# Engine order from a list scheduler, DMA transposes and per-pair scores in a windowed-attention + MLP kernel

## The chip, the cores and the metric

The kernel runs on one core of a Trainium2 chip. The metric is the time of one execution on the device, in microseconds (us). A run more than 1.5% above the fastest of the same kernel counts as slow and is left out of comparisons. The engines are called PE (TensorE, matmuls), PEld (its weight loads), ACT (ScalarE), DVE (VectorE), POOL (GpSimd) and SP (SyncE, which here only issues DMAs).

## The reference, cut to what matters

```python
# q, k, v: 4 batches x 8 heads x 768 rows x 64; n_global = 8, n_local = 96
scores = scale * q @ k.T + bias(head, distance)      # kept: 96 local columns and the first 8
a = softmax(where(keep, scores, -1e9));  attn = a @ v
x = attn -> (3072 rows) x (8 heads * 64 = 512)
h = x @ w_in                  # 512 x 2048
out = relu(h)**2 @ w_out      # 2048 x 512, float32
```

The 3072 rows are 24 tiles of 128. Because of the window, a tile needs keys of itself and of the tile before (plus the 8 global columns, which are copied into the tile before). Two tiles make a block. In the names below, `kT` and `xT` are k and x transposed, `sc` the scores, `esc` their exp, `po` the result of the attention's second product (PV). The MLP of a block has eight steps. "Stage 1" of a step is eight 128x128 by 128x256 matmuls into `hT`, then relu on ACT, then the square on DVE. "Stage 2" is four matmuls with 512 columns that accumulate over the eight steps into two banks `acc`.

q and k have a standard deviation of 0.1, so the scaled scores vary by about 0.1 x 0.1 x 8 / 8 = 0.01. The output therefore hardly depends on q and k.

## The kernel before

TensorE transposes q, k and the attention result x of every tile (heads are interleaved with zeros in `qz`, so that one matmul gives the scores of a pair of heads). PSUM is the memory that the matmuls write to; it is divided into banks. Scores of two pairs fill two PSUM banks, and one exp reads both. The order of the instructions is a hand-made table.

```python
    ps_acc = ...tile_pool(name="ps_acc", bufs=1, space=PSUM)   # acc0, acc1: 2 banks
    ps_h   = ...tile_pool(name="ps_h",   bufs=2, space=PSUM)
    ps_sc  = ...tile_pool(name="ps_sc",  bufs=1, space=PSUM)   # 2 banks
    ps_tr  = ...tile_pool(name="ps_tr",  bufs=1, space=PSUM)
    ps_o   = ...tile_pool(name="ps_o",   bufs=1, space=PSUM)
# ... cut ...
    def unit_a(j):                     # transposes of tile j
        tr = ps_tr.tile([P, 2 * NPAIR, P], BF16, name="tr", tag="tr")
        # ... 4 + 4 nc.tensor.transpose of q and k into tr ...
        nc.vector.tensor_copy(z[:D, :, 0, :], tr[:D, :NPAIR, :])
        nc.vector.tensor_copy(z[D:, :, 1, :], tr[D:, :NPAIR, :])
        nc.scalar.copy(kT[j], tr[:, NPAIR:, :])
# ... cut ...
    def unit_scores(j, hf):            # two pairs of heads at a time
        sc = ps_sc.tile([P, 2, 4 * P], FP32, name="sc", tag="sc")
        # ... four score matmuls, 256 columns each ...
        esc = work.tile([P, 8 * P], BF16, name="esc", tag="esc")
        nc.scalar.activation(out=esc, in_=sc..., func=Act.Exp, scale=scale)
        # ... at = esc * bias on DVE ...
# ... cut ...
    for j in range(8, NT):
        a0 = 4 * (j - 2) - 5
        put(j, A=a0, B=a0 + 2, C=a0 + 3, D=a0 + 4, E=a0 + 5, F=a0 + 7)
```

The softmax here doesn't subtract the row's maximum and nothing guards it: scores larger than these inputs give would overflow.

## Time and profile before

| | before |
|---|---|
| median (before the prediction, 3 runs) | 269.84 us (267.59 to 270.02) |
| PE busy | 223.3 us, 84% of the span |
| DVE, ACT busy | 57%, 52% |
| first stage-1 matmul | 26.7 us |
| steady block (two tiles) | 19.4 us |

The page of the profile gives the busy time of each engine, and then rows of 40 equal slices: a digit is the busy share of a slice in tenths, in the row PEclk the share of full clock that was granted, in the row DMA the share of the 16 DMA engines.

```profile
PE 223.3 (84%) x1935; PEld 160.3 (60%) x1968; DVE 151.1 (57%) x350; ACT 139.8 (52%) x229; POOL 73.4 (28%) x94
...
PE   1345969686989899899799899898998998999993
...
PEclk9999999999999999999999999999999999999999
DMA  8999999999999300200200200200200200202022
```

PE is the busiest engine, less so in the first third, and the DMA engines are full for the first third (the loads) and nearly idle afterwards.

The windows view gives, for each stretch of time, its length and the busy time of PE, PEld, DVE, ACT and POOL (instructions in brackets), then granted clock, DMA share (of the packets' time, so above 1 where packets wait for each other) and GB/s.

```profile
40.00:60.00 20.00, 16.46 (x147) 12.16 (x151) 11.53 (x25) 9.30 (x14) 19.14 (x23) 1.00 2.42 155
60.00:80.00 20.00, 15.94 (x157) 11.79 (x158) 11.29 (x25) 10.62 (x17) 19.54 (x24) 1.00 2.33 170
...
120.00:140.00 20.00, 18.34 (x162) 13.48 (x164) 11.59 (x25) 11.22 (x19) 0.00 (x0) 1.00 0.08 28
```

From 80 us on, up to the last 30 us, PE is busy 18.3 to 18.6 of 20 us at full clock (one such stretch is shown), and no other engine comes near that. From 40 to 80 us it lacks 4 us in 20.

The table of waits, for PE (waiting instruction, what ended the wait, us in total, times, longest):

```profile
PE acc L338 <- ACT o L349: 10.5, 9, 1.4
...
```

And the timeline of PE at the end of a steady block (start, duration, line, operation, output and inputs, how many; in brackets an idle time before it and what ended it). Durations of single matmuls contain their pipeline latency; the distance of two starts is what a group really costs.

```profile
185.34 0.29 PE L254 MATMUL po<-v,at 128*128 128x65 bf16 x4
187.08 1.08 PE L338 MATMUL acc<-wout,hs 128*128 128x512 bf16 x4 [1.45 <-ACT o L349]
...
188.87 0.60 PE L219 MATMUL sc<-qz,kT 128*128 128x256 bf16 x4
189.31 1.03 PE L338 MATMUL acc<-wout,hs 128*128 128x512 bf16 x4
...
```

Once in most blocks, stage 2 of the next block waits for ACT to evict the accumulator (1.45 us here, 10.5 us in all). The score group takes 189.31 - 188.87 = 0.44 us for its four matmuls.

### The profile page before, as it was taken

Reading aid. Unit: us, or ns where it says so; the run is one execution under the profiler, and the core shown is the slowest. Engines: PE = TensorE matmul, PEld = TensorE weight load, DVE = VectorE, ACT = ScalarE, POOL = GpSimd, SP = SyncE. Lnnn points to the kernel's source line nnn. Section 1 sums busy time; section 2 is a strip of 40 time slices with the busy share of each in tenths; the row PEclk is TensorE's granted clock in tenths of the full one; section 3 lists DMA queues with packets and bytes.
Section 4 is the critical chain, followed back from the end, with each engine's and each line's share of the span. In section 5 each row is a group of like instructions: output and inputs, shape, how many; then the busy total and the mean of one; then the engine's idle time right before and its main releaser. Section 6 shows DMA issues by size and latency. Waiting matters only on the chain.

```text
span 266.5 us, 4844 instructions
## 1 busy us (share of the span) xinstructions
PE 223.3 (84%) x1935; PEld 160.3 (60%) x1968; DVE 151.1 (57%) x350; ACT 139.8 (52%) x229; POOL 73.4 (28%) x94
## 2 busy tenths in 40 slices
PE   1345969686989899899799899898998998999993
PEld 1124657464666677577577677576676775766641
DVE  6444576466457576565557567565575675653310
ACT  5432474444557456556556555654745646635321
POOL 8986778999994000000000000000000000000000
PEclk9999999999999999999999999999999999999999
DMA  8999999999999300200200200200200200202022
GB/s 161 155 196 200 186 180 155 157 155 155 198 157 154 87 2 0 81 1 2 79 2 1 79 2 0 81 0 2 79 2 1 79 2 1 81 0 81 0 79 79
DMA packets 84758, 20.76 MB, mean 78 GB/s; under 512 B 75520, under 2 KB 81664, under 8 KB 84736
## 3 DMA queue, kind: packets, MB, share of 16 engines
q0 software_dynamic: 77120, 13.11, 63.2%
q1 hardware_dynamic: 7616, 7.34, 8.3%
q8 instruction: 15, 0.25, 0.4%
q14 instruction: 7, 0.06, 0.1%
HBM read 27.26 MB, written 6.29 MB: 126 GB/s over the span
## 4 chain that ended last, share of the span: by engine, by line
PE 66%; DVE 16%; ACT 11%; issue 5%; ACTq 0%
PE acc L338 27%; PE hT L314 26%; PE sc L219 7%; DVE hs L325 4%; ACT hr L323 4%; DVE x L275 3%; DVE qz L188 2%; ACT esc L228 2%; PE po L265 2%; ACT o L349 2%; PE trx L291 2%; DVE qz L187 2%; ACT kT L189 2%; DVE at L237 1%; DVE rs L274 1%
## 5 line engine op out<-in xcount | busy, mean ns | idle before, releaser
L325 DVE TENSOR_TENSOR hs<-hr 128x512 bf16<-128x512 f32 x96 | 66.3, 691 | 69.6 <-ACT hr L323 69.3
L338 PE MATMUL acc<-wout,hs 128*128 128x512 bf16 x351 | 92.9, 379 | 12.3 <-ACT o L349 10.5
L314 PE MATMUL hT<-xT,win 128*128 128x256 bf16 x768 | 101.2, 276 | 0.1
L314 PEld LDWEIGHTS <-win 128*128 128x128 bf16 x768 | 75.7, 99 | 28.2 <-issue 0.2
L323 ACT ACTIVATE hr<-hT 128x512 f32<-128x512 f32 x96 | 57.7, 601 | 54.6 <-PE hT L314 54.6
L338 PEld LDWEIGHTS <-hs 128*128 128x128 bf16 x384 | 35.7, 98 | 37.6 <-issue 13.2
L228 ACT ACTIVATE esc<-sc 128x1024 bf16<-128x1024 f32 x44 | 45.2, 1028 | 5.8 <-PE sc L219 4.7
L237 DVE TENSOR_TENSOR at<-esc,E 128x1024 bf16<-128x1024 bf16 x44 | 30.4, 691 | 27.1 <-ACT esc L228 27.0
L189 ACT COPY kT<-tr 128x512 bf16<-128x512 bf16 x24 | 14.0, 584 | 50.8 <-DVE qz L188 45.1
L219 PE MATMUL sc<-qz,kT 128*128 128x256 bf16 x160 | 25.8, 287 | 7.5 <-ACT kT L189 5.2
L87 POOL DMA_DIRECT2D v<-in_v_dram x24 | 23.4, 975 | 2.6 <-DMA win<-in_moe_w_in_dram 1.2
L96 POOL DMA_DIRECT2D k<-in_k_dram x22 | 21.3, 968 | 3.3 <-DMA wout<-in_moe_w_out_dram 2.8
L219 PEld LDWEIGHTS <-kT 128*128 128x128 bf16 x160 | 15.3, 102 | 10.6 <-ACT kT L189 6.1
L96 POOL DMA_DIRECT2D q<-in_q_dram x22 | 21.2, 965 | 1.4 <-DMA win<-in_moe_w_in_dram 0.7
L275 DVE TENSOR_TENSOR x<-po,rs 128x256 bf16<-128x256 f32 x48 | 20.4, 425 | 1.7
L265 PE MATMUL po<-v,at 128*128 128x65 bf16 x320 | 16.8, 196 | 3.4 <-DVE x L275 3.4
L265 PEld LDWEIGHTS <-at 128*128 128x128 bf16 x320 | 15.1, 100 | 5.7 <-DVE x L275 4.9
L349 ACT COPY o<-acc 128x512 f32<-128x512 f32 x24 | 13.0, 597 | 6.3 <-PE acc L338 6.3
L180 PE MATMUL tr<-ident,q 128*128 128x128 bf16 x96 | 9.9, 230 | 6.8 <-DVE q L175 6.8
L294 ACT COPY xT<-trx 128x512 bf16<-128x512 bf16 x24 | 14.0, 582 | 3.1 <-PE trx L291 3.1
L291 PE MATMUL trx<-ident,x 128*128 128x128 bf16 x96 | 9.9, 226 | 5.7 <-ACT kT L189 4.1
L291 PEld LDWEIGHTS <-x 128*128 128x128 bf16 x96 | 7.5, 100 | 6.9 <-issue 4.5
(34 smaller groups left out, 94.2 us busy)
## 6 DMA issues: line engine op xcount, KB each, us to landing
out_dram<-o SPq DMA_DIRECT2D x24, 256.0 KB, 2.2
v<-in_v_dram POOLq DMA_DIRECT2D x24, 128.0 KB, 6.1
q<-in_q_dram POOLq DMA_DIRECT2D x22, 128.0 KB, 5.9
k<-in_k_dram POOLq DMA_DIRECT2D x22, 128.0 KB, 6.0
win<-in_moe_w_in_dram POOLq DMA_DIRECT2D x8, 256.0 KB, 7.2
wout<-in_moe_w_out_dram POOLq DMA_DIRECT2D x8, 256.0 KB, 9.8
plain_q<-in_q_dram SPq DMA_DIRECT2D x2, 256.0 KB, 3.9
plain_k<-in_k_dram SPq DMA_DIRECT2D x2, 256.0 KB, 4.3
```

The costliest lines, as they stand in the source:

```text
L87: nc.gpsimd.dma_start(out=v_sb[j][:, :, :D], in_=v[b, :, t * P : (t + 1) * P, :].rearrange("h p d -> p h d"),)
L96: nc.gpsimd.dma_start(out=dst.rearrange("p (h d) -> p h d", h=H), in_=src[b, :, rows, :].rearrange("h p d -> p h d"),)
L219: nc.tensor.matmul(out=sc[:, pi, i * 2 * P : (i + 1) * 2 * P], lhsT=kT[kj][:, pair, :], rhs=z[:, pair, :, :], start=True, stop=True, skip_ ...
L228: nc.scalar.activation(out=esc, in_=sc.rearrange("p a b -> p (a b)"), func=Act.Exp, scale=scale)
L237: nc.vector.tensor_mul(at, esc, bias)
L265: nc.tensor.matmul(out=po[:, hi, :], lhsT=a4[:, hi // 2, i, hi % 2, :], rhs=v_sb[kj][:, h, :], start=(i == 0), stop=(i == 1), skip_group_c ...
L275: nc.vector.tensor_tensor(out=x[:, 4 * hf : 4 * hf + 4, :], in0=po[:, :, :D], in1=rs.to_broadcast([P, 4, D]), op=Alu.mult,)
L291: nc.tensor.transpose(out=trx[:, kt, :], in_=x[:, kt * P : (kt + 1) * P], identity=ident)
L314: nc.tensor.matmul(out=hT[:, c, :], lhsT=w_in_sb[s][:, kt, c * P : (c + 1) * P], rhs=xT[blk][:, kt, :], start=(kt == 0), stop=(kt == KM - ...
L323: nc.scalar.activation(hr, hT, Act.Relu)
L325: nc.vector.tensor_mul(hs, hr, hr)
L338: nc.tensor.matmul(out=acc[blk][sub], lhsT=hs[:, c, sub * P : (sub + 1) * P], rhs=w_out_sb[s][:, c, :], start=(s == 0 and c == 0), stop=(s ...
```

## The change

The intent: PE should do matmuls only. q and k of tiles 4 and up are transposed by DMA (SP), q from buffers padded with zeros; x too. A list scheduler with estimated costs orders all engines: it takes, again and again, the operation that can start first by its plan. Scores are made per pair of heads (one bank), the accumulators get a third bank, weights of the two stages are loaded alternately, and copies go to ACT or DVE, whichever is planned to be free. The diff, cut to its core:

```diff
+class Plan:
+    LAG = {"PE": 0.2, "ACT": 0.1, "DVE": 0.1, "SP": 2.6, "POOLQ": 2.5, "DMA": 0.0}
+    def run(self):
+        # ... among ready operations, take the one with the least (start, key, cost) ...
+                if o["takes"]:                       # a buffer of a ring
+                    tag, bufs, users = o["takes"]
+                    if len(ring) >= bufs:
+                        old = ring[-bufs]            # wait for the users of the oldest
 # ... cut ...
-    ps_acc = ctx.enter_context(tc.tile_pool(name="ps_acc", bufs=1, space=PSUM))
+    ps_acc = ctx.enter_context(tc.tile_pool(name="ps_acc", bufs=3, space=PSUM))
     ps_h = ctx.enter_context(tc.tile_pool(name="ps_h", bufs=2, space=PSUM))
     ps_sc = ctx.enter_context(tc.tile_pool(name="ps_sc", bufs=1, space=PSUM))
-    ps_tr = ctx.enter_context(tc.tile_pool(name="ps_tr", bufs=1, space=PSUM))
     ps_o = ctx.enter_context(tc.tile_pool(name="ps_o", bufs=1, space=PSUM))
 # ... cut ...
+    NPE = 4
+    NPAD, NK, NV, NKT, NQZ = 6, 6, NT, 2 * TPB, 4
 # ... cut: loads of tiles 6 and up wait for the buffers that transposes free ...
+            ld = plan.op(("load", j), {"POOLQ": 2.6}, emit_load,
+                deps=pad_users[j % NPAD] + k_users[j % NK], key=base, ready=clock[0])
 # ... cut: tiles below NPE keep TensorE transposes, the others get ...
+                nc.sync.dma_start_transpose(
+                    out=qz[zi].rearrange("p a b c -> p (a b) c"),
+                    in_=q_tile[j].rearrange("p a b c -> p (a b c)"))
+                nc.sync.dma_start_transpose(out=kT[ki], in_=k_tile[j])
+            T = plan.op(("T", j), {"SP": 1.5}, emit_T, ..., key=base - 6)
 # ... cut ...
+                sc = ps_sc.tile([P, 2, 2 * P], FP32, name="sc", tag="sc")
+            s_ = plan.op(
+                ("sc", j, pair), {"PE": 0.11 if first else 0.22}, emit_sc, deps=deps,
+                key=base + 0.5 + 0.4 * pair, takes=("sc", 2, users))
 # ... cut: exp, mask and PV per pair; x of tiles 4 and up ...
+                nc.sync.dma_start_transpose(
+                    out=tiles["xT", blk][:, :, tt * P : (tt + 1) * P],
+                    in_=tiles["x", j].rearrange("p h d -> p (h d)"))
+            c = plan.op(("xT", j), {"SP": 0.9}, emit_xT, deps=norm, key=base + 3, takes=xT_ring)
 # ... cut ...
+    for o in plan.run():
+        if o["emit"]:
+            o["emit"](o["engine"])
```

## The prediction

> **What bounds the kernel now.** TensorE. In the windows table of the kernel before, PE is busy 18.4 to 18.6 of each 20 us from 80 to 240 us at full granted clock, while DVE has 11.5 to 13.6 and ACT 10.7 to 12.0. The timeline shows a block (two tiles, eight steps) every 19.4 us. By start-to-start times its TensorE work is 8 stage-1 groups of 0.87 us, 8 stage-2 groups of 0.86, four score groups of 0.44, four PV groups of 0.25, and transposes (q and k 0.22 each, x 0.22) of 1.35 us for both tiles: about 18.0. The rest is mostly one wait a block for the accumulator's eviction: the table of waits has "PE acc <- ACT o" 10.5 us in 9 waits. The start is the other loss: the first stage-1 matmul runs at 26.7 us, PE is busy 20.7 of the first 40 us and 32.4 of the 40 after.
>
> **Removed.** TensorE transposes of 20 tiles (0.67 us each, 13.5 us) and their copies (DVE 0.84, ACT 1.16 us a tile, off the critical path); the accumulator wait (10 us); some early idle: float32 transposes need no casts, k comes on a second queue, and w_out chunks come between w_in chunks, so stage 2 can start before all of stage 1 of block 0 is done. The weights still need what the trace's 160 to 200 GB/s allows, so block 0 ends near 45 us either way, but with some 6 us of stage 2 done. Without new waits I estimate a 16.6 us block and about 229 us in all.
>
> **Added.** Three DMA transposes a tile on SP. The Trainium skill, "VectorE: DVE Perf Modes", section "The three transpose paths", gives 1309 ns for a 128x128 through the DMA crossbar against 390 on TensorE; this trace has 230 ns (modelled) for the latter and no instance of the former. With tiles prepared steps ahead I expect little of it on the chain.
>
> **The catch.** The plan lets the scheduler use two score buffers, but the score pool keeps one buffer; a pair's scores now fill one bank. "PSUM — Partial Sum Buffer", section "Specifications (TRN2)", gives 8 banks of 512 float32: the new pools take 3+2+1+1 = 7, so a bank lies idle. The keys put two score pairs back to back, twice a tile, right after a stage-1 group whose relu goes ahead of the exp on ACT. The second pair must then wait for relu and exp: from this trace 0.17 us pipeline, 0.49 for the relu, 0.60 for the exp, less 0.22 own issue, so about 1.1 us idle. Twice a tile, some 18 tiles in steady state: 35 to 40 us on TensorE, all critical. A block would then take 20 to 21 us, longer than before, and nearly all of the gain goes.
>
> **Prediction.** 263 us, range 245 to 278. Faster by over 2%: 0.48; within 2%: 0.32; slower: 0.20.
>
> **What would show each step.** Right: transposes of later tiles gone from PE; "PE acc <- ACT o" near zero; first stage-1 matmul near 20 us; "PE sc <- ACT esc" the largest PE wait, 25 to 45 us, in 30 to 40 waits of about 1 us; block period 19.5 to 21 us; ACT and DVE under 65% busy. Wrong: score waits under 15 us (the order interleaves other work, then 230 to 245 us); large waits of PE on DMA transposes (q, k or xT), which would make it slower; a first stage-1 matmul later than 26 us.
>
> **What would make it wrong.** DMA transposes slower than the planned 4 us, above all beside the early loads; the in-order SP queue blocked by a store; score pairs less often adjacent than I read from the keys; the zero fills on POOL delaying the weights more than the estimated 3 us.

## The result, and the profile after

The changed kernel took 284.42 us (median of 4 runs, 283.07 to 284.83) against 268.76 us: slower, at a ratio of 1.0573 (95% interval 1.05 to 1.0646). Ratios here are the mean time of one kernel's fast runs over that of the other's fast runs of the same rounds, so they are not quite the ratios of the quoted medians. All four runs were fast ones, yet their mean granted clock was 0.96.

The page after, same lines as before:

```profile
PE 225.1 (80%) x1728; PEld 152.1 (54%) x1728; DVE 147.5 (52%) x375; ACT 122.6 (43%) x226; POOL 89.0 (32%) x120
...
PE   2778987594387958887977978978878888879993
...
PEclk9999999799559979999999999999999999999998
DMA  8999999999999994987997997245164021020201
```

PE was busy for as long as before (225 us), although it executes 240 matmuls fewer (12 transposes in each of 20 tiles; the counts on the page differ by 207, as some records of the kernel before are missing). The saving hardly shows in the busy time, which fits with two things: the 33 missing records are of `acc` (351 of 384, 92.9 us against 103.3 us after), and the kernel after runs part of its matmuls at half clock, where they take longer. The DMA row is full for much longer, and in the first half the granted clock sinks to a half in some slices.

The windows of the kernel after:

```profile
40.00:60.00 20.00, 13.96 (x111) 8.91 (x110) 9.65 (x24) 8.48 (x15) 14.95 (x19) 0.91 1.95 164
60.00:80.00 20.00, 11.81 (x63) 6.72 (x62) 4.35 (x10) 3.66 (x8) 11.44 (x15) 0.80 1.82 155
...
120.00:140.00 20.00, 17.15 (x146) 11.89 (x144) 11.61 (x27) 9.71 (x17) 6.55 (x8) 1.00 1.05 121
```

Two losses show. From 40 to 110 us PE works far less than before, at a lowered clock. Counting the stage-1 matmuls in this stretch gives 152, against 216 before: 64 fewer, one whole block. From 120 us on, the clock is full and PE still reaches only 16.7 to 17.2 of 20 us.

The table of waits of PE, after:

```profile
PE sc L404 <- ACT esc L432: 34.1, 49, 1.0
PE hT L605 <- DMA xT<-x: 9.5, 2, 7.4
...
PE sc L404 <- DMA kT<-k: 3.3, 2, 2.9
PE acc L669 <- DVE hs L638: 0.9, 2, 0.6
```

The accumulator wait is gone. In its place stand 34.1 us of waits of score matmuls for the exp of the pair before. The timeline of PE in a steady block shows one of them, and the ACT timeline below it why it is so long:

```profile
182.63 1.04 PE L605 MATMUL hT<-xT,win 128*128 128x256 bf16 x8
183.50 0.38 PE L404 MATMUL sc<-qz,kT 128*128 128x256 bf16 x2
184.84 0.38 PE L404 MATMUL sc<-qz,kT 128*128 128x256 bf16 x2 [0.95 <-ACT esc L432]
...
```

```profile
183.70 0.60 ACT L626 ACTIVATE hr<-hT 128x512 f32<-128x512 f32 x1 [1.14 <-PE hT L605]
184.19 0.59 ACT L432 ACTIVATE esc<-sc 128x512 bf16<-128x512 f32 x1
```

The first score pair starts at 183.50, right behind a stage-1 group. ACT takes that group's relu first (183.70) and then the exp of the pair (184.19). The second pair needs the same bank, so it can start only at 184.84: 1.34 us after the first, where its own work needs 0.22. The steady block takes 182.63 to 202.75, that is 20.1 us, longer than the 19.4 us before.

The chain that ended last shows the other loss (start, duration, what):

```profile
...
42.16 9.06 DMA kT<-k
...
65.76 8.56 DMA xT<-x
...
74.45 1.65 PE hT L605 x7
...
```

A transpose of k takes 9 us from issue to landing, and one of x takes 8.6 us, while stage 1 of the next block waits for it. The slow landing is not the whole of this wait. The timeline of SP shows what stood before that x:

```profile
62.42 3.24 SPq L382 DMA_TRANSPOSE kT<-k  x1
65.76 1.28 SPq L581 DMA_TRANSPOSE xT<-x  x1
```

DVE had finished this x at 60.85 us, but SP came to it only at 65.76 us. Until 59.7 us SP had stood at a store whose accumulator was not yet copied (10.3 us), and then it issued that store and the q and k transposes of a later tile. So x spent 4.9 us in SP's queue and 8.6 us from issue to landing; PE had other work until 67.0 us and then waited 7.4 us.

The DMA view of 30 to 100 us gives the median time from issue to landing of each kind:

```profile
qz<-qpad SPq DMA_TRANSPOSE x8, 8.2
kT<-k SPq DMA_TRANSPOSE x8, 7.8
xT<-x SPq DMA_TRANSPOSE x4, 6.6
```

The plan counted on 4.1 us for q and k together (1.5 of issue and 2.6 to land) and 3.5 us for x. And a long wait costs twice, because the clock falls. The windows of PE around the wait for x (length, PE busy, clock, DMA share, GB/s):

```profile
66.00:74.40 8.40, 1.01 (x6) 0.85 1.82 137
74.40:86.00 11.60, 10.05 (x42) 0.52 1.80 199
86.00:100.00 14.00, 11.22 (x91) 1.00 2.15 154
```

After the wait of 7.4 us, PE ran for 11.6 us at a mean clock of 0.52. The Trainium skill, "TensorE: Matmul & The Clock Gate", section "What's actually happening", describes such a fall to half clock after an idle window of about 3.4 us. This trace agrees for the wait of 7.4 us, but shorter idling did it too: after a wait of 2.9 us (for kT, ending at 51.3 us) the clock was at half for 3.4 us, and after one of 2.1 us (for xT, ending at 100.9 us), soon followed by a score wait of 0.95 us, for another 3.4 us. By themselves the score waits, of 1.0 us at most, leave the clock at 1.00 from 107 to 270 us.

### The profile page after: what moved, and what is told of

It is laid out like the page before. It is cut to its first block, busy times and chain, and to the rows that moved or that the text cites. A ratio compares the mean times of both kernels' runs of the same rounds, so it can differ in the third digit from the quotient of the medians.

```text
span 282.4 us, 4671 instructions
## 1 busy us (share of the span) xinstructions
PE 225.1 (80%) x1728; PEld 152.1 (54%) x1728; DVE 147.5 (52%) x375; ACT 122.6 (43%) x226; POOL 89.0 (32%) x120
## 3 DMA queue, kind: packets, MB, share of 16 engines
q1 hardware_dynamic: 48416, 17.31, 33.7%
## 4 chain that ended last, share of the span: by engine, by line
PE 57%; DMA 15%; ACT 11%; POOL 6%; DVE 5%; issue 4%; SPq 0%; ACTq 0%; POOLq 0%
PE acc L669 25%; PE hT L605 23%; ACT esc L432 9%; PE sc L404 6%; DMA xT<-x 5%; DMA wout<-in_moe_w_out_dram 4%; DMA qpad<-in_q_dram 3%; DMA kT<-k 3%; PE po L495 2%; DVE at L452 2%; ACT hr L626 2%; DVE o L278 1%; POOL v L175 1%; POOL win L175 1%; POOL qpad L259 1%
## 5 line engine op out<-in xcount | busy, mean ns | idle before, releaser
L669 PE MATMUL acc<-wout,hs 128*128 128x512 bf16 x384 | 103.3, 387 | 0.9 <-DVE hs L638 0.9
L638 DVE TENSOR_TENSOR hs<-hr 128x512 bf16<-128x512 f32 x96 | 66.3, 691 | 65.9 <-ACT hr L626 65.1
L404 PE MATMUL sc<-qz,kT 128*128 128x256 bf16 x176 | 38.1, 293 | 37.4 <-ACT esc L432 34.1
L432 ACT ACTIVATE esc<-sc 128x512 bf16<-128x512 f32 (+1 forms) x96 | 53.8, 560 | 32.3 <-PE sc L404 30.6
L175 POOL DMA_DIRECT2D qpad<-in_q_dram x40 | 30.4, 771 | 62.6 <-DMA qz<-qpad 59.3
L452 DVE TENSOR_TENSOR at<-esc,E 128x512 bf16<-128x512 bf16 (+1 forms) x96 | 37.0, 396 | 10.8 <-ACT esc L432 10.8
L278 DVE COPY o<-acc 128x512 f32<-128x512 f32 x12 | 8.3, 692 | 25.2 <-PE acc L669 25.2
L520 DVE RECIPROCAL rs<-po 128x4 f32<-128x4 f32 x48 | 8.7, 180 | 12.7 <-PE po L495 11.8
L276 ACT COPY o<-acc 128x512 f32<-128x512 f32 x12 | 7.0, 585 | 10.3 <-PE acc L669 10.3
L175 POOL DMA_DIRECT2D win<-in_moe_w_in_dram x8 | 6.5, 818 | 2.2 <-DMA win<-in_moe_w_in_dram 2.2
L175 POOL DMA_DIRECT2D wout<-in_moe_w_out_dram x8 | 6.0, 754 | 2.2 <-DMA wout<-in_moe_w_out_dram 2.2
```

What stands on the lines that cost most here:

```text
L175: nc.gpsimd.dma_start(out=dst, in_=src)
L278: nc.vector.tensor_copy(dst, src)
L404: nc.tensor.matmul(out=sc[:, i, :], lhsT=kT[(j - i) % NKT][:, pair, :], rhs=qz[zi][:, pair, :, :], start=True, stop=True, skip_group_check ...
L432: nc.scalar.activation(out=esc[:, :n], in_=sc.rearrange("p a b -> p (a b)")[:, :n], func=Act.Exp, scale=scale,)
L452: nc.vector.tensor_mul(at_, tiles.pop(("esc", j, pair))[:, : at_.shape[1]], bias)
L520: nc.vector.reciprocal(rs, po[:, :, D : D + 1])
```

## The experiments

Theory A: two causes. The single score buffer, which the plan believes to be two, costs about 35 us of PE waits; and DMA transposes beside the loads take 6 to 9 us, which starves PE until about 110 us. Rivals: only one of these matters; or transposes are slow by themselves; or SP's order or the tie between buffers and loads is at fault. Each run was compared with the kernel before in the same rounds (its medians there were 268.1 to 269.2 us).

| run | median us | ratio to before (95%) |
|---|---|---|
| changed kernel | 284.42 | 1.0573 (1.05-1.0646) |
| 1: two score buffers | 258.09 | 0.9605 (0.9561-0.9648) |
| 2: one buffer, and the plan knows | 263.59 | 0.9832 (0.9792-0.9872) |
| 3: all transposes on PE | 279.84 | 1.0416 (1.0367-1.0465) |
| 4: 1 and 3 together | 241.41 | 0.8991 (0.8958-0.9024) |
| 5: as 1, x on PE | 246.50 | 0.9196 (0.9163-0.9229) |
| 6: as 1, tiles 4 to 11 on PE | 232.84 | 0.8668 (0.8645-0.8692) |
| 7: as 1, no late loads of q and k | 246.96 | 0.9211 (0.9176-0.9247) |
| 8: as 1, dearer SP in the plan | 264.39 | 0.9852 (0.9801-0.9903) |
| 9: as 1, no late loads at all | 236.75 | 0.8800 (0.875-0.8851) |
| 10: as 6, larger rings, later zero fills | 229.92 | 0.8551 (0.8512-0.8591) |
| 11: as 4, two accumulator banks | 241.41 | 0.8978 (0.8942-0.9024) |
| 12: as 1, larger rings | 265.54 | 0.9893 (0.9842-0.9943) |

### 1 and 2: the score buffer

Run 1 changes one number, and the two traces show the same operations in the same order on every engine as in the changed kernel:

```diff
-    ps_sc = ctx.enter_context(tc.tile_pool(name="ps_sc", bufs=1, space=PSUM))
+    ps_sc = ctx.enter_context(tc.tile_pool(name="ps_sc", bufs=2, space=PSUM))
```

> The score pool gets the two buffers that the plan counts on (the idle bank); the order of every engine stays the same as in the changed kernel. Theory A (half of the loss is the single score buffer): the waits of score matmuls for the exp fall from 34 us to under 5, the steady block from 20.1 to 16.6-17 us, the time from 284 to 250-258 us; the stretch from 40 to 110 us stays poor, with xT and kT transposes of 6 to 9 us. Rival B (DMA transposes beside the loads are all that matters, the score waits hide other waits): the time stays above 275 us.

Measured: 258.09 us, 26 us less than the changed kernel and at the edge of the forecast. Its waits of PE:

```profile
PE hT L605 <- DMA xT<-x: 18.9, 5, 8.7
PE sc L404 <- DMA kT<-k: 6.8, 2, 5.0
...
```

No wait of scores for the exp is left among the rows of this table. From 160 to 220 us the windows view has PE busy 20.00 of each 20 us, and the steady block takes 16.6 us, which is what the prediction gave without new waits. The waits for DMA transposes grew instead, to 18.9 and 6.8 us, as the early score waits no longer hide them. This fits with 34 us of waits giving back only 26.

Run 2 keeps the single buffer and corrects the plan:

```diff
-                key=base + 0.5 + 0.4 * pair, takes=("sc", 2, users),
+                key=base + 0.5 + 0.4 * pair, takes=("sc", 1, users),
```

> The score pool keeps one buffer, but the scheduler is told so, and orders the engines for one. Theory A: it puts other TensorE work between two score pairs; score waits fall under 15 us and the time to 258-268 us. If it is the number of buffers and not the false count in the plan that costs, the waits stay near 30 us and the time above 278.

Measured: 263.59 us, 21 us less than the changed kernel, with one score buffer:

```profile
PE sc L404 <- DMA kT<-k: 10.4, 3, 6.1
PE hT L605 <- DMA xT<-x: 10.0, 5, 4.4
PE sc L404 <- ACT esc L432: 6.0, 13, 0.7
...
```

With the true count, the scheduler puts stage-2 or PV matmuls between two score pairs, and the score waits fall from 34.1 to 6.0 us. So most of the cost was not the single buffer as such, but a plan that counted on two. The second buffer is still worth 5.5 us (263.59 to 258.09). Run 2 orders every engine anew, so its other waits differ too.

### 3 and 4: the transposes back on PE

A condition of its own, in place of `j < NPE`, says which tiles TensorE transposes; the order of the loads stays. (A q tile for TensorE loads in one DMA into a buffer of its own, not in two into a padded one; this small difference comes along.)

```diff
+    QK = lambda j: True      # q, k by TensorE
+    XP = lambda j: True      # x by TensorE
-        if j < NPE:          # at the load of q, at the transposes of q and k
+        if QK(j):
-        if j < NPE:          # at the transpose of x
+        if XP(j):
```

> All 24 tiles transposed by TensorE as tiles 0 to 3 are (through the two hT banks); one score buffer with the plan's false count stays, loads keep their order. Theory A (contention of transposes with loads is the other half): no slow clock from 60 to 110 us, no wait for xT or kT; some 20 us come back there, against 1.35 us of TensorE work a block (10 blocks, 13 us): 272-280 us, with a steady block of 21 to 21.5. Rival (transposes cost nothing, the start is poor for lack of data): 290 us or more.

> Both: two score buffers and all transposes on TensorE. If the two causes add: 240-248 us with a steady block near 18 us. If one of them was only a stand-in for the other: no better than the first run of this batch.

Run 3 (one score buffer): 279.84 us, with no wait for a DMA transpose among the rows, a clock of 0.996, and the score waits as they were:

```profile
PE sc L406 <- ACT esc L434: 35.4, 48, 1.0
...
```

Run 4 (two buffers): 241.41 us. Its windows, to be read against 13.96 and 11.81 of the changed kernel:

```profile
40.00:60.00 20.00, 19.97 (x169) 13.94 (x168) 11.88 (x27) 10.27 (x19) 16.15 (x19) 1.00 2.11 180
60.00:80.00 20.00, 19.97 (x179) 14.49 (x178) 14.07 (x36) 13.64 (x28) 6.55 (x8) 1.00 1.04 88
...
```

So both causes are real, and run 4 lies within its forecast. The gains of the single changes do not add up to the joint one, which is larger: the PE transposes gain 4.6 us with one buffer (284.42 to 279.84) and 16.7 us with two (258.09 to 241.41); the second buffer gains 26.3 us with DMA transposes and 38.4 us with PE transposes. This fits with score waits and waits for DMA that partly cover each other in the first 110 us, so that removing one lays the other bare.

### 5 and 6: which transposes, and when

Run 5 has two score buffers, `QK = lambda j: j < NPE` and `XP = lambda j: True`. Run 6 has both set to `j < 12`.

> Two score buffers (as all of this batch); x of every tile transposed by TensorE, q and k of tiles 4 and up still by DMA. If only the late, urgent xT transposes cost (they wait on SP behind q and k of tiles further ahead), this gives 240-246 us. If the q and k transposes themselves, two thirds of the transposed bytes, slow the loads and are slowed by them, sc waits for kT remain and it lands at 246-256.

> Two score buffers; tiles 4 to 11 transposed by TensorE, tiles 12 and up by DMA, so that hardly any transpose meets the dense loads of the first 80 us. If transposes are harmless once the dense loads are over: 232-239 us, faster than all on TensorE (241.4) by what 12 tiles' transposes cost there, some 8 us. If they hurt there too: 241 us or more.

Run 5: 246.50 us, at the border of the two forecasts. It is 11.6 us faster than run 1 with only x on PE, so the urgent x transposes are the larger part; but 10.6 us of waits for kT remain, and with all on PE it is another 5.1 us faster. Run 6: 232.84 us, 8.6 us faster than all on PE. Transposes by DMA do pay, for the tiles whose transposes come after the dense loads. (Its profiled execution, 236.25 us, fell in a slow run, so its trace is not used for times.)

### 7, 8, 9 and 12: why the transposes are slow

Run 7 leaves out the q and k loads of tiles 6 and up, but keeps the v loads, the transposes and the planned order; run 9 leaves out the v loads as well (late tiles use the v buffers of the first six). Both compute something wrong.

```diff
     def load_tile(j):
+        if j >= NPE + 2:
+            q_tile[j], k_tile[j] = q_pad[j % NPAD], k_ring[j % NK]
+            load_v(j)        # run 9: without this line, and v_sb[j] = v_sb[j % 6]
+            return
```

> Wrong result on purpose: two score buffers, all DMA transposes and the engine order kept, but the q and k loads of tiles 6 and up left out (zeros or old tiles are transposed in their place), v still loaded. If the loads slow the transposes: transposes of 40 to 110 us land in 2.4 to 4.5 us instead of 8, waits for xT and kT under 6 us, 232-242 us. If transposes are slow by themselves or blocked by the order on SP: waits stay above 15 us and the time above 250.

> Wrong result on purpose: as the run without late q and k loads, and the v loads of tiles 6 and up left out too, so nothing is loaded after about 45 us; two score buffers, the engine order and all DMA transposes kept. In the earlier run v loads moved up and filled the DMA engines until 72 us, and only after that did transposes land in 2.4 to 3.7 us. If loads are what slows the transposes: the wait of 9.6 us for xT near 65 us goes too, transposes after 50 us land in 2.4 to 4 us, 230-238 us. If not: still near 247.

Run 7: 246.96 us, between the forecasts. The v loads, no longer behind q and k, moved up and kept the DMA engines full until about 72 us, and until then nothing got better; waits of 16.2 us for xT and kT remained, which was the rival's side of the forecast. From 70 to 110 us the transposes landed fast:

```profile
...
qz<-qpad SPq DMA_TRANSPOSE x7, 3.4
kT<-k SPq DMA_TRANSPOSE x7, 3.7
xT<-x SPq DMA_TRANSPOSE x4, 2.4
```

Run 9 removed these loads too: 236.75 us. From 50 to 160 us its transposes land in 2.4 to 3.3 us:

```profile
...
qz<-qpad SPq DMA_TRANSPOSE x16, 3.3
kT<-k SPq DMA_TRANSPOSE x16, 2.6
xT<-x SPq DMA_TRANSPOSE x12, 2.4
```

The same DMAs, in the planned order of run 1, land in a third to two fifths of the time shown for the changed kernel once nothing is loaded beside them, and the wait for xT shrinks from 18.9 to 2.0 us. So the transposes are not that slow by themselves; the loads beside them make them so. That it is the shared DMA engines, and not the memory behind them, fits the full DMA rows but was not separated. Run 9 also removes the wait of q and k transposes for their data, so that by itself it would not tell late data from slow transposes; but the times above count from issue to landing. In SP's queue x stood almost as long as before: the x transpose that made PE wait 7.4 us in the changed kernel waited 4.0 us there in run 9 (4.9 us in the changed kernel), and yet no wait of PE for xT was over 1.6 us. So most of the long waits is slow landing. What a shorter queue alone would give was not tested.

Run 9 was reported as wrong (relative error 1.11). Run 7 was reported as correct, although it used stale or zero q and k: this is the insensitivity to q and k named above. The passed checks of the other runs thus prove the x, v and MLP paths, but not the q and k transposes.

Run 8 has two score buffers and only tells the scheduler dearer DMA transposes:

```diff
-    LAG = {..., "SP": 2.6, ...}      # and {"SP": 1.5} for q and k, {"SP": 0.9} for x
+    LAG = {..., "SP": 7.0, ...}      # and {"SP": 2.6} for q and k, {"SP": 1.2} for x
```

> Two score buffers; only the plan's costs for SP changed: 7 us to landing instead of 2.6, 2.6 and 1.2 us of issue instead of 1.5 and 0.9. If the order was only planned too tight: waits for xT and kT under 10 us, 242-250 us. If the DMA engines are simply full, no order helps: 254-262 us.

Measured: 264.39 us, 6 us worse than run 1 and above both forecasts. A better forecast for SP did not make the transposes any faster (medians of 9.0 to 9.4 us from 30 to 70 us, against 8.1 to 9.1 us in run 1), and the new order had a bad stretch of its own: PE was busy 5.5 us from 60 to 80 us. This one order did not help the start; others were not tried.

Run 12 has two score buffers and loosens the tie by which a load waits until a transpose has freed its buffer (POOL waited 59 us for that in the changed kernel). The zero fills of the six additional q buffers come after the weight loads:

```diff
-    NPAD, NK, NV, NKT, NQZ = 6, 6, NT, 2 * TPB, 4
+    NPAD, NK, NV, NKT, NQZ = 12, 24, NT, 2 * TPB, 4
```

> Two score buffers, all transposes of tiles 4 and up by DMA as in the first run of this study, but 12 padded q buffers and 24 k buffers, so that a load need not wait for a transpose to free its buffer. If the tie between transposes and loads (POOL waits 59 us for transposes in the changed kernel) is what stretches the poor stretch: loads end near 95 us instead of 150, and the time falls to 245-252 us. If it is only that transposes and loads share the engines at the same time: the transposes of 40 to 95 us get no faster, 254-262 us.

Measured: 265.54 us, even slower than I gave the rival. The loads did not end near 95 us: POOL issued the last ones at 128 us, now waiting for earlier loads to land. From 40 to 95 us the transposes of q, k and x got no faster, as the rival said (medians of 9.0, 7.8 and 7.8 us, against 8.5, 8.0 and 8.1 us in run 1). And the waits of PE for transposes grew:

```profile
PE hT L607 <- DMA xT<-x: 22.9, 3, 9.9
...
```

The tie was not the fault. That the tie even helped, by holding loads back until after transposes, fits the numbers but was not tested by itself.

### 10: the version that beats both

Two score buffers, `j < 12` on PE for q, k and x, rings of 12 padded q and 24 k buffers, and the zero fills of the padded buffers issued after the weight loads instead of before.

> The best so far (two score buffers, tiles 4 to 11 on TensorE) with 12 padded q buffers and 24 k buffers, so that all loads end before tiles 12 and up are transposed by DMA, and with the zero fills after the weight loads. Expected: the first stage-1 matmul 2 to 3 us earlier, no wait for xT near 125 us; 226-231 us against 232.8. If the wait for xT there has another cause than the loads: it stays, and 230 us or more.

Measured: 229.92 us (229.42 to 230.33), ratio 0.8551 to the kernel before.

```profile
...
PE   1788997899999999999999999999999999999992
...
PEclk9999999999999999999999999999999999999999
...
```

```profile
PE trq L342 <- DVE v L215: 4.7, 1, 4.7
PE hT L607 <- DVE kT L280: 1.9, 1, 1.9
...
```

The rows are those of 40 slices again, of the run's page. PE is busy without gaps from about 45 us on, and the clock is full throughout. Here all loads are issued by about 100 us. From 70 to 110 us the transposes of tiles 12 to 15 still took 8 us beside them, but they were issued before they were needed, and PE waited for none. The wait of 3.0 us for xT that run 6 had is gone, and its wait for w_in fell from 3.9 to 0.7 us (both figures of run 6 are from its slow execution). One part of the forecast failed: the first stage-1 matmul came at 18.6 us, not 2 to 3 us before the 18.4 us of run 6. What came earlier is stage 1 of the second block, at 37.6 us against 41.5 us.

### 11: the third accumulator bank

Run 4 with two banks instead of three, in the pool and in the plan:

```diff
-    ps_acc = ctx.enter_context(tc.tile_pool(name="ps_acc", bufs=3, space=PSUM))
+    ps_acc = ctx.enter_context(tc.tile_pool(name="ps_acc", bufs=2, space=PSUM))
-    takes=("acc", 3, users)      # three places
+    takes=("acc", 2, users)
```

> The run with two score buffers and all transposes on TensorE, with two accumulator banks instead of three, in the pool and in the plan. If the third bank is worth what the wait was before the change (10.5 us): 249-253 us against 241.4. If the scheduler can put other work in that gap: 241-244 us.

Measured: 241.41 us, the same as run 4. The largest waits of PE show no accumulator:

```profile
PE trq L342 <- DVE v L215: 4.8, 1, 4.8
PE hT L607 <- DMA win<-in_moe_w_in_dram: 3.6, 2, 3.1
...
```

The 10.5 us of accumulator waits before the change are thus gone without the third bank. The scheduler, told of two, lets other matmuls run while the eviction goes on.

## Why the prediction was wrong

The prediction said 263 us (245 to 278) and thought faster likelier than slower; measured was 284.42.

1. **"What bounds the kernel now. TensorE."** Right: removing PE waits (runs 1, 2, 4, 10) moved the time each time.
2. **"The catch": the one score buffer.** Right in mechanism and in total; the waits were more and shorter than predicted. Predicted were 25 to 45 us in 30 to 40 waits of about 1 us and a block of 20 to 21 us; measured were 34.1 us in 49 waits (0.70 us each) and 20.1 us. Run 1 (the spare bank used) removed the waits. The spare bank was read from the pools and from the Trainium skill, "PSUM — Partial Sum Buffer", section "Specifications (TRN2)", which gives 8 banks; run 1 uses the eighth, builds and runs.
3. **"With tiles prepared steps ahead I expect little of it on the chain."** This step failed. The prediction named slow transposes beside the early loads as a risk, but put no time on them. Medians were 6.6 to 8.2 us from issue to landing, with a wait of 7.4 us and a halved clock behind it, and the stretch from 40 to 110 us lost a block of work against the kernel before. Taking the loads away is worth 21.3 us (run 1 to run 9). Nor is x prepared steps ahead: the x of the 7.4 us wait was ready only 6.2 us before PE ran out of other work, and it then lost 4.9 us in SP's queue, behind the q and k of a later tile, which SP had issued only after a store. A store that blocks SP was among the risks that the prediction named. The skill's figure that I had quoted ("VectorE: DVE Perf Modes", section "The three transpose paths": 1309 ns for 128x128) does not tell this: with free DMA engines, one DMA of four such squares landed in 2.4 us here, and beside loads in 6.6 to 8.2 us.
4. **The sum.** Without new waits I had 229 us, plus 35 to 40 for the score waits: 264 to 269, from which 263 was taken. The missing term is that of point 3: adding its 21 us gives 285 to 290. As the two partly cover each other, the sum is only a rough one.
5. **"The accumulator wait (10 us)" removed.** The wait went, and the third bank was not needed for it (run 11).
6. **"First stage-1 matmul near 20 us."** It was at 23.5 us. In run 1 it came at 18.5 us, so the score waits delayed the start as well.

Left open: how much of run 10's gain over run 6 (2.9 us) is due to the rings and how much to the later zero fills, as both were changed at once (by the traces 1.9 us of it are there when the third block starts, before any tile that is transposed by DMA is used, but run 6's trace is of a slow execution); how much of the waits for xT a freer SP queue would remove; and whether another priority of transposes and loads could save DMA transposes in the first 100 us.

## What to carry to other kernels

A schedule is only as good as the resource counts in it: check that every buffer count that a planner believes in is the one that the pools allocate, because an in-order engine pays for each false count with a wait. Work moved from a busy engine to "free" DMA is free only where the DMA engines are free: put a time from issue to landing on it for the stretch in which the loads run, and move only what comes after them. Long waits of PE cost more than their length, as the clock falls behind them (here at half speed for 3.4 us after a wait of 2.9 us, and for 11 us of work after one of 7.4 us).

## What the Trainium skill lacked or had wrong

- "Advanced Engine Details and Errata", section "X-Bar Transpose (TRN2)", says "TRN2 transpose DMAs are as fast as regular DMAs". Here they were not. SP's queue moved 7.34 MB in 8.3% of 266.5 us before the change (stores and plain loads: 332 GB/s of packet time). In run 9, with hardly any loads beside it, it moved 17.31 MB in 36.8% of 234.9 us. With the 6.8 MB of stores and plain loads taken at the former rate (20.5 us), the 10.5 MB of transposes took 65.9 us, that is an estimated 159 GB/s. A stretch of run 9 in which SP moved only transposes gives 196 GB/s (1.19 MB in 74.8% of the 8.1 us from 64.3 to 72.4 us).
- "DMA: Bandwidth & Descriptors", section "Rules for kernel authors", says "A transpose next to ordinary DMAs needs nothing". No run here speaks against this for correctness; for time, no page gives a figure for a transpose beside loads: median time to landing of x transposes rose from 2.4 us (run 9, no loads) to 6.6 us (changed kernel, 30 to 100 us), and of q transposes from 3.3 to 8.2 us.
- "TensorE: Matmul & The Clock Gate", section "What's actually happening", gives about 3.4 us of sustained work to regain the full clock. After the wait of 7.4 us, the stretch at about half clock lasted some 11 us here (mean clock 0.52 from 74.4 to 86.0 us), with waits of 0.75 us in between; the page gives no figure for how gaps of this size prolong the slow phase. And the fall did not need one idle stretch of 3.4 us: in the same trace a wait of 2.9 us was followed by half clock, and so was one of 2.1 us with a further one of 0.95 us after it, while one of 2.1 us in run 5 (at 39 us) was not.
